# Retention and MoE on one core: chunk 1's loads over two hardware queues, chunk 2's k ahead of its q blocks, and M1(0) in four PSUM banks

## The chip, the core and the metric

The kernel runs on one core of a Trainium2 chip. The metric is the device time of one execution in microseconds (us), as a median over runs. Where a profile is read, times are microseconds from the start of its span, which is about 1.8 us shorter than the device time of the same execution. Engines go by the profile's names: PE is TensorE, PEld its weight loads, DVE VectorE, ACT ScalarE, POOL GpSimd, SP SyncE. A q behind a name (SPq, ACTq) marks the issue of DMAs; L419 is line 419 of that kernel's source, and x8 means eight instructions merged.

## The reference, cut to what matters

Two stages, one after the other. The first is a retention recurrence per batch and head, the second a two-layer MLP on its output:

```
B, H, S, D = 4, 8, 768, 64
state = gamma * state + k[t] v[t]^T            # per batch and head, gamma per head
y[t]  = q[t] . state / sqrt(D)
x     = y as (B*S, H*D) = (3072, 512)
out   = gelu_tanh(x @ w_in) @ w_out            # 512 -> 2048 -> 512
```

## The kernel before

The sequence is cut into six chunks of 128 tokens. For each chunk and each of the four batches the kernel makes the transposes T of q and k, the scores A, the output y and the state update S. Then the MLP runs over the chunk's 512 tokens: M1 (x @ w_in, 16 blocks "fc" of 128 columns, with gelu) and M2 (g @ w_out, four batches, each in units of four matmuls). "M1(1)" is M1 of chunk 1, "T(1,0)" the transposes of chunk 1, batch 0. The attention of the next chunk is woven into M1 and M2 of this one. PSUM is shared out in banks:

```python
BANKS = {"h": 2, "o": 2, "att": 4}        # M1, M2, attention: eight in all

def moe1_two(c, fp, t0, t1):              # two fc blocks for tokens t0..t1
    h_ps = bank("h", shape=(128, 2, B * C // 2), name="h_ps")
    for r in range(2):
        moe1_mm(c, 2 * fp + r, h_ps[:, r, 0:t1 - t0], t0, t1)
    gelu(g_tile(c, 2 * fp)[:, :, t0:t1], h_ps[:, :, 0:t1 - t0])
```

The loads of chunk 1 stand after M1(0) in the program. `hold` keeps the first q load back until the third piece of w_out has landed:

```python
hold("q", 1, 0, w_out_sb[2][0:1, 0, 0:1])
for fc in range(8, NF):                   # rest of M1(0)
    moe1(0, fc)
    if fc in (9, 11):
        load1(AC, "v", 1, (fc - 9) // 2)  # v(1,0), v(1,1) from ScalarE
...                                       # q and k by turns, all from SyncE
load1(AC, "v", 1, 2)
load1(AC, "v", 1, 3)
u = [units2(0, b, tag="ooho"[b]) for b in range(B)]   # M2(0)
run([u[i % 3][i // 3] for i in range(12)] + u[3], {8: [(preps, 1, 0)], 10: [(att_T, 1, 0), ...], ...})
load_blk("q", 2)                          # 16 DMAs of 64 KB, each for all four batches
for b in range(B):
    load1(SY, "k", 2, b)
...                                       # late outputs of chunk 0, v of chunk 2
```

From chunk 2 on q comes in blocks, which VectorE transposes itself, so POOL's scaling of q for any batch waits for all 16 block loads.

## Time and profile before

| | before |
|---|---|
| time | 216.12 us (216.09 to 216.35, 4 runs) |
| span of the profile | 215.2 us |
| TensorE (PE) busy | 206.6 us, 96% |
| PE's waits after 15 us | 0.79 (w_in), 0.24 (gelu), 1.37 (o bank) us |
| M1(1) starts, M2(1) starts | 52.55, 70.37 us |

The lines behind this are shown in the prediction. A bracket at the end of a timeline line gives the idle time just before it and what ended it.

### The profile page before, as it was taken

How to read it: one execution, taken by the hardware profiler on the slowest of the kernel's cores; microseconds unless marked ns; L12 is line 12 of the kernel's file. 1: busy time of each engine (PE TensorE's matmuls, PEld its weight loads, DVE VectorE, ACT ScalarE, POOL GpSimd, SP SyncE). 2: the span in 40 equal slices, each digit the busy share in tenths (PEclk: the TensorE clock that was granted, in tenths of full speed). 3: DMA queues.
4: the chain of work that ended last, by engine and by line, in shares of the span. 5: the costliest groups of instructions: out<-in, count | busy, mean ns of one | idle time of the engine just before them, and what ended most of it. 6: DMA issues, size and time to landing. Idle time of an engine off the chain costs nothing.

```text
span 215.2 us, 3935 instructions
## 1 busy us (share of the span) xinstructions
PE 206.6 (96%) x1551; PEld 113.5 (53%) x1551; DVE 86.4 (40%) x156; ACT 86.6 (40%) x149; POOL 96.5 (45%) x117
## 2 busy tenths in 40 slices
PE   7898999979999999999999999999999999999992
PEld 2466744447888655444545444545444544444461
DVE  5667000188755553217672235673235640100000
ACT  2456671054555223366123376123375113565110
POOL 2997100234279553569743799211499221100000
PEclk9999999999999999999999999999999999999998
DMA  6999999896799687899688998879920012100121
GB/s 153 288 234 207 206 205 229 198 250 111 155 227 282 109 161 146 173 286 187 101 159 166 280 207 130 125 147 221 296 57 0 0 61 88 49 0 0 52 97 49
DMA packets 124801, 32.78 MB, mean 152 GB/s; under 512 B 118064, under 2 KB 122928, under 8 KB 124784
## 3 DMA queue, kind: packets, MB, share of 16 engines
q1 hardware_dynamic: 107840, 20.48, 48.4%
q0 software_dynamic: 6112, 8.65, 17.2%
q10 hardware_dynamic: 10832, 3.41, 6.7%
q8 instruction: 12, 0.20, 0.4%
q14 instruction: 5, 0.04, 0.1%
HBM read 30.44 MB, written 6.29 MB: 171 GB/s over the span
## 4 chain that ended last, share of the span: by engine, by line
PE 76%; DMA 14%; POOL 3%; SPq 2%; ACT 1%; issue 0%; ACTq 0%; DVE 0%
PE o_ps L452 33%; PE h_ps L419 32%; DMA w_out<-in_moe_w_out_dram 9%; DMA k<-in_k_dram 5%; PE y_ps L307 3%; PE a_ps L272 3%; SPq L98 2%; PE y_ps L294 2%; PE s_ps L326 2%; POOL w_in L400 1%; PE qkT_ps L249 1%; POOL k L195 1%; DMA out_dram<-o_sb 1%; POOL w_out L409 1%; ACTq L98 0%
## 5 line engine op out<-in xcount | busy, mean ns | idle before, releaser
L452 PE MATMUL o_ps<-w_out,g 128*128 128x512 f16 (+1 forms) x400 | 88.1, 371 | 1.4 <-ACT o_sb L474 1.4
L419 PE MATMUL h_ps<-xT,w_in 128*128 128x512 f16 (+2 forms) x496 | 86.7, 331 | 1.1 <-DMA w_in<-in_moe_w_in_dram 0.8
L434 ACT ACTIVATE g<-h_ps 128x512 f16<-128x512 f32 (+1 forms) x98 | 57.5, 588 | 48.7 <-PE h_ps L419 48.6
L419 PEld LDWEIGHTS <-w_in 128*128 128x128 f16 x496 | 46.3, 98 | 37.0 <-DMA w_in<-in_moe_w_in_dram 1.0
L452 PEld LDWEIGHTS <-g 128*128 128x128 f16 x400 | 37.7, 98 | 40.2 <-issue 1.4
L285 DVE TENSOR_TENSOR a_sb<-a_ps,mask 128x512 f16<-128x512 f32 x48 | 30.1, 683 | 14.5 <-PE a_ps L272 14.4
L195 POOL TENSOR_TENSOR k<-k,cst 128x512 f16<-128x512 f32 x24 | 25.1, 1045 | 16.2 <-DMA k<-in_k_dram 16.1
L479 POOL DMA_DIRECT2D out_dram<-o_sb x17 | 9.6, 567 | 42.9 <-ACT o_sb L474 33.3
L474 ACT COPY o_sb<-o_ps 128x512 f32<-128x512 f32 x19 | 11.0, 586 | 41.6 <-PE o_ps L452 38.4
L352 POOL TENSOR_TENSOR stg<-st,cst 128x512 f32<-128x512 f16 x16 | 16.5, 1042 | 11.1 <-DVE st L343 9.7
L343 DVE TENSOR_TENSOR st<-s_ps,stg 64x256 f16<-64x256 f32 x32 | 13.5, 421 | 17.8 <-PE s_ps L326 17.2
L206 POOL TENSOR_TENSOR q<-q,cst 128x512 f16<-128x512 f32 x16 | 16.7, 1046 | 3.2 <-DMA q<-in_q_dram 3.2
L258 DVE STREAM_TRANSPOSE qkT<-q 128x512 f16<-128x512 f16 x16 | 11.2, 702 | 13.9 <-POOL q L206 13.7
L195 DVE TENSOR_TENSOR q<-q,cst 128x512 f16<-128x512 f32 x8 | 6.6, 826 | 21.9 <-DMA q<-in_q_dram 21.9
L231 ACT CAST xT<-y_ps 128x512 f16<-128x512 f32 x15 | 8.3, 588 | 12.0 <-PE y_ps L307 12.0
L206 POOL TENSOR_TENSOR kT<-kT,cst 128x512 f16<-128x512 f32 x12 | 12.5, 1044 | 0.5 <-issue 0.5
L171 PE MATMUL spin_ps<-zero 128*128 128x512 f16 x31 | 9.7, 456 | 1.3 <-DVE zero L139 1.3
L491 DVE COPY o_sb<-o_ps 128x256 f32<-128x256 f32 x1 | 0.4, 425 | 25.2 <-PE o_ps L452 25.2
L192 POOL CAST v<-v 128x512 f16<-128x512 f32 x16 | 9.6, 606 | 0.5 <-DMA v<-in_v_dram 0.4
L190 ACT CAST v<-v 128x512 f16<-128x512 f32 x7 | 4.3, 621 | 12.7 <-issue 10.8
L258 DVE STREAM_TRANSPOSE qkT<-kT 128x512 f16<-128x512 f16 x12 | 8.3, 694 | 2.6 <-POOL kT L206 2.6
L272 PE MATMUL a_ps<-qkT 64*128 64x128 f16 x192 | 8.1, 218 | 0.7 <-ACT qkT L231 0.7
(36 smaller groups left out, 95.1 us busy)
## 6 DMA issues: line engine op xcount, KB each, us to landing
k<-in_k_dram SPq DMA_DIRECT2D x22, 256.0 KB, 4.6
v<-in_v_dram SPq DMA_DIRECT2D x18, 256.0 KB, 4.7
out_dram<-o_sb POOLq DMA_DIRECT2D x17, 256.0 KB, 3.1
q<-in_q_dram SPq DMA_DIRECT2D x64, 64.0 KB, 2.7
kT<-in_k_dram SPq DMA_DIRECT2D x48, 64.0 KB, 2.8
w_out<-in_moe_w_out_dram POOLq DMA_DIRECT2D x4, 512.0 KB, 17.6
q<-in_q_dram SPq DMA_DIRECT2D x6, 256.0 KB, 5.5
v<-in_v_dram ACTq DMA_DIRECT2D x6, 256.0 KB, 7.6
```

Source lines behind the costliest of these rows:

```text
L171: nc.tensor.matmul(out=ps, lhsT=zero[:, 0:128], rhs=zero, start=True, stop=True)
L195: eng.tensor_tensor(out=t, in0=src, in1=cst[:, col:col + H].unsqueeze(2).broadcast_to([128, H, Dh]), op=ALU.mult,)
L206: nc.gpsimd.tensor_tensor(out=t, in0=ld_all((key, c))[:, b * NHP:(b + 1) * NHP].rearrange("p hp a d -> p (hp a) d"), in1=cst[:, col:col + ...
L258: nc.vector.transpose(out=t[:, i].rearrange("p hp t -> p (hp t)"), in_=blk16.pop((nm, c, b)).rearrange("p ha d -> p (ha d)"),)
L272: nc.tensor.matmul(out=ps[j][:, hp], lhsT=t[j * 64:(j + 1) * 64, 1, hp], rhs=t[j * 64:(j + 1) * 64, 0, hp], start=True, stop=True,)
L285: nc.vector.tensor_tensor(out=s, in0=ps[j], in1=mask[:, j], op=ALU.mult)
L343: eng.tensor_tensor(out=st[sl, :, b, sl], in0=s_ps[sl, :, sl], in1=stg[sl, :, b, sl], op=ALU.add,)
L352: nc.gpsimd.tensor_tensor(out=stg[:, :, b], in0=st[:, :, b], in1=cst[:, OG:OG + NHP].unsqueeze(2).broadcast_to([128, NHP, 128]), op=ALU.mult,)
L419: nc.tensor.matmul(out=out, lhsT=w_in_sb[wi][:, kc, wr * 128:(wr + 1) * 128], rhs=xT[c][:, kc, t0:t1], start=(kc == 0), stop=(kc == NHP - ...
L434: nc.scalar.activation(out=out, in_=in_, func=AF.Gelu_apprx_tanh, scale=1.0)
L452: nc.tensor.matmul(out=ps[:, n0:n1], lhsT=g_sb[c, fc // 2][:, fc % 2, b * C:(b + 1) * C], rhs=w_out_sb[fc // (NF // NO)][:, fc % (NF // NO ...
L474: nc.scalar.copy(out=o_sb, in_=ps)
```

## The change

The intent is to take out PE's last idle times before 60 us. The loads of chunk 1 go over both hardware queues so that nothing blocks ScalarE while it should empty M2's banks. M1(0) gets four banks and another order, so that it need not wait for a gelu or for w_in. Chunk 2's k goes ahead of its q blocks.

```diff
-    def moe1_two(c, fp, t0, t1):
-        h_ps = bank("h", shape=(128, 2, B * C // 2), name="h_ps")
+    def moe1_two(c, fp, t0, t1, tag="h"):
+        h_ps = bank(tag, shape=(128, 2, B * C // 2), name="h_ps")
...
-    moe1_two(0, 1, *t01)          # before y(0,2)
     mm_yc(0, 2, "o")
     mm_yi(0, 2)
     ev_Y(0, 2)
     mm_s(0, 2)
+    moe1_two(0, 1, *t01)
...
-    (pairs 1 to 3 in parts of 256 and 128 tokens, fc 8 to 15 whole)
+    moe1_two(0, 1, *t2, "o")
+    moe1_two(0, 0, *t3)
+    moe1_two(0, 1, *t3, "o")
...
-    for fc in range(8, NF):
+    for fc in range(4, NF):
...
-    load1(SY, "q", 1, 0)          # q and k by turns, all SyncE
-    load1(SY, "k", 1, 0)
-    ...
-    load1(AC, "v", 1, 2)
-    load1(AC, "v", 1, 3)
+    for b in range(B):
+        load1(SY, "q", 1, b)
+    for b in range(B - 1):
+        load1(AC, "k", 1, b)
+    load1(SY, "k", 1, 3)
+    load1(SY, "v", 1, 2)
+    load1(SY, "v", 1, 3)
...
-    load_blk("q", 2)
     for b in range(B):
         load1(SY, "k", 2, b)
+    load_blk("q", 2)
...                                # POOL: all k, all q, all v, in place of q and k by turns
```

More of the change, by code (lines that the diff above doesn't have):

```diff
@@ L573 @@
     moe1_two(0, 0, *t2)
-    moe1_two(0, 1, *t2)
-    moe1_two(0, 2, *t01)
+    moe1_two(0, 1, *t2, "o")
+    moe1_two(0, 0, *t3)
+    moe1_two(0, 1, *t3, "o")
     ev_S(0, 2)
     ev_S(0, 3)
-    moe1_two(0, 3, *t01)
-    moe1_two(0, 0, *t3)
-    moe1_two(0, 1, *t3)
-    for fp in range(2, 4):
-        moe1_two(0, fp, half, 2 * half)
     for b in range(B):
@@ L603, in preps @@
         prep1(AC, "v", c, b)
-    load1(SY, "q", 1, 0)
-    load1(SY, "k", 1, 0)
-    load1(SY, "q", 1, 1)
-    load1(SY, "k", 1, 1)
-    load1(SY, "q", 1, 2)
-    load1(SY, "k", 1, 2)
-    load1(SY, "q", 1, 3)
+    for b in range(B):
+        load1(SY, "q", 1, b)
+    for b in range(B - 1):
+        load1(AC, "k", 1, b)
     load1(SY, "k", 1, 3)
-    load1(AC, "v", 1, 2)
-    load1(AC, "v", 1, 3)
+    load1(SY, "v", 1, 2)
+    load1(SY, "v", 1, 3)
     u = [units2(0, b, tag="ooho"[b]) for b in range(B)]
@@ L636 @@
         load1(SY, "v", 2, b)
-    for b in range(B):
-        prep_blk("q", 2, b)
-        prep1(PO, "k", 2, b)
-    for b in range(B):
-        prep1(PO, "v", 2, b)
+    for nm in "kqv":
+        for b in range(B):
+            prep_blk("q", 2, b) if nm == "q" else prep1(PO, nm, 2, b)
     run(
```

## The prediction

> **What bounds the kernel now.** I read the page first, for who is busy.
>
> ```profile
> span 215.2 us, 3935 instructions
> PE 206.6 (96%) x1551; PEld 113.5 (53%) x1551; DVE 86.4 (40%) x156; ACT 86.6 (40%) x149; POOL 96.5 (45%) x117
> ```
>
> TensorE (PE) is busy 96% of the span, and the chain that ended last runs through its matmuls from 45 us to the end. So a microsecond taken out of PE's stream before that point is worth a microsecond at the end, unless a later wait takes it back. All that can be won is PE's idle time. The table of waits, cut to PE and to 15 to 62 us, lists all of it:
>
> ```profile
> PE o_ps L452 <- ACT o_sb L474: 1.4, 1, 1.4
> PE h_ps L419 <- DMA w_in<-in_moe_w_in_dram: 0.8, 1, 0.8
> PE h_ps L419 <- ACT g L434: 0.2, 1, 0.2
> ```
>
> The columns are total, count, longest. From 62 us on PE never waits. The timeline of PE shows where these three sit (start, length, instruction, idle before):
>
> ```profile
> 17.50 1.05 PE L419 MATMUL h_ps<-xT,w_in 128*128 128x256 f16 x8 [0.79 <-DMA w_in<-in_moe_w_in_dram]
> 18.48 0.41 PE L307 MATMUL y_ps<-a_sb,v 128*64 128x128 f16 x8
> 18.83 0.62 PE L326 MATMUL s_ps<-v,k 128*128 128x128 f16 x8
> ...
> 19.73 3.44 PE L419 MATMUL h_ps<-xT,w_in 128*128 128x128 f16 x40
> 23.41 9.26 PE L419 MATMUL h_ps<-xT,w_in 128*128 128x128 f16 x56 [0.24 <-ACT g L434]
> 32.51 9.66 PE L452 MATMUL o_ps<-w_out,g 128*128 128x512 f16 x44
> 42.00 0.39 PE L249 MATMUL qkT_ps<-iden,q 128*128 128x128 f16 x4
> ...
> 45.24 1.02 PE L452 MATMUL o_ps<-w_out,g 128*128 128x512 f16 x4 [1.37 <-ACT o_sb L474]
> ```
>
> The first wait is M1(0) (the first MoE matmul of chunk 0) for its second w_in piece, the second for a gelu to free an M1 bank, the third for ScalarE (ACT) to empty the bank that M2's last batch takes. Why ACT was late is in its timeline and in SyncE's:
>
> ```profile
> 38.77 0.85 SPq L98 DMA_DIRECT2D k<-in_k_dram  x1
> ...
> 43.02 1.02 ACTq L98 DMA_DIRECT2D v<-in_v_dram  x2
> 44.08 0.62 ACT L190 CAST v<-v 128x512 f16<-128x512 f32 x1 [10.78 <-issue]
> 44.61 1.07 ACT L474 COPY o_sb<-o_ps 128x512 f32<-128x512 f32 x2
> ```
>
> ACT's in-order stream holds two v loads ahead of the v cast and the copy. The order of instructions with their waits shows that the hardware-queue DMAs share eight completion semaphores, and that the first of these v loads waits for k(1,1), issued at 38.77, to land; the chain of waits has that at 42.94. ACT stands still for 10.78 us and then works off what was ready long before.
>
> Last, what feeds chunk 1: the timeline of GpSimd (POOL) shows when each k landed.
>
> ```profile
> 40.66 1.04 POOL L195 TENSOR_TENSOR k<-k,cst 128x512 f16<-128x512 f32 x1 [5.99 <-DMA k<-in_k_dram]
> 43.01 1.04 POOL L195 TENSOR_TENSOR k<-k,cst 128x512 f16<-128x512 f32 x1 [1.31 <-DMA k<-in_k_dram]
> ```
>
> k(1,0) is ready at 40.66 + 1.04 = 41.70, and PE takes its transpose at 42.00. This edge has only 0.3 us of slack, which matters below.
>
> **What the Trainium skill says.** "DMA: Bandwidth & Descriptors", section "Issuing engines are not separate DMA queues": DMAs from several engines run on the same 16 DMA engines, so a second queue saves only the time to start them. The trace half agrees: the prologue, on both queues, moved 284 GB/s from 7 to 12 us, and SyncE's queue alone reached 264 in 42 to 44, so the ceiling is near the same. But in 38 to 40 us the single queue gave only 119 GB/s, between one slow issue (2.99 us) and the next. Two queues should fill such holes, not raise the ceiling. The same page, "Queues, rings and completion order", says that each DMA engine takes turns between the queue rows that have work. That decides who comes first below; the trace agrees for the prologue, where loads of the two queues landed in turn about 0.9 us apart. "PSUM — Partial Sum Buffer", "Specifications (TRN2)", gives 8 banks per partition: the kernel holds 2 for M1, 2 for M2, 4 for attention, so M1 can have a third and fourth bank only by borrowing M2's, idle in this stage once y is evicted.
>
> **The change, part by part.**
> (a) M1(0) of pair 1 moves behind y(0,2) and s(0,2). Those are 0.35 us and 0.22 us of PE work (8 and 4 matmuls; the rows at 18.48 and 18.83 are spaced 0.35, and 8 s matmuls take 0.55 to the next). Their inputs are there by 16.8 us, and w_in only at 17.46. They fill 0.57 of the 0.79 us hole.
> (b) Four single-batch groups (8 matmuls of 128 columns each) come directly after one another, with M2's two banks for every second one, so four banks are in use and no gelu has to end first. Before, the 40 matmuls from 19.73 hold 2 x 8 x 0.109 + 3 x 8 x 0.055 = 3.06 us by their steady spacing, yet the next group starts 3.68 later: 0.6 us is really lost at the gelu, more than the 0.24 the table gives, since the ends of matmuls are modelled.
> (c) fc 4 to 7 run as 16 matmuls of 512 columns in place of 32 of 256: 16 x 0.216 = 3.45 against 32 x 0.109 = 3.49 us. That is nothing. Four 512-wide gelus stay four.
> Sum of (a) to (c): from 17.50, PE now has 0.98 (pair 1) + 0.22 (s) + 0.35 (y) + 1.76 (four single-batch groups) + 12 x 0.863 (fc 4 to 15) = 13.7 us, so M2(0) starts near 31.2 in place of 32.5: **1.3 us**. w_in and w_out pieces still come in time.
> (d) That lead meets the loads. M2(0) runs 11 units of 0.863 us and reaches T(1,0) (the transposes of chunk 1) at 40.7. k(1,0) now goes out from ACT behind v(1,0) and v(1,1), without the hold; but until 38 us the engines are full (277 GB/s from 36 to 38), and in front of it are the same bytes: w_out, two v, and q(1,0) by turns. So I put its landing at 40.6 again, k16 ready at 41.7, T(1,0) at about 41.75. Of the 1.3 us, **0.3 is left** here; 1.0 becomes a new wait of PE for k.
> (e) Behind ACT's k loads stand the v cast and the copies. The third, k(1,2), waits for q(1,0) to land (near 39.7), is out by 40.6, and the copy of M2's first batch ends by 41.7, while PE wants the bank at 43.4. The 1.37 us wait (1.44 by spacing: 43.80 to 45.24) is gone: **1.4 us**. From T(1,0) on PE has 10.55 - 1.44 = 9.1 us of work up to M1(1), which starts at 41.75 + 9.1 = 50.9 in place of 52.55: **1.7 us** so far.
> (f) The last v loads, now on SyncE behind q and k, each wait for an earlier q in the ring of semaphores: v(1,3) is issued near 45.1 and lands near 49.3 (4.2 us from issue, like k(1,1)), against 49.47 before. ACT casts it, copies u3 and evicts y(1,1) by 50.9: exactly when PE wants it. No gain and perhaps 0.2 lost.
> (g) Chunk 2: k loads first (4 x 0.9 us from 46), then 16 q blocks at 0.6 us each from 49.6, landed near 62. POOL now does k, then q: the second q is ready at 62 + 2 x 1.04 = 64.1, VectorE transposes and evicts by 65.0. PE wants A(2,0) and A(2,1) at 66.81 - 1.7 = 65.1. Cost 0 to 0.5; I take 0.2.
> Sum: 0.3 + 1.4 - 0.2 = 1.5, so 216.12 - 1.5 = **214.6 us**.
>
> **Rivals.** First, **the k and q loads keep up**: both rows alternate and k(1,0), already queued, goes ahead of q(1,0). It could land near 39.7; then step (d) keeps up to 1 us more and the time is 213.7. For it: the hole of 38 to 40 us. Against: full engines until 38. Second, **a new wait at the late loads**: v(1,3) or the q blocks come 1 us later than I reckon, as they are last in one queue. M1(1) or A(2,0) then gives back what was won: 215.4 to 215.8. For it: (f) and (g) have next to no slack. Third, **the bank borrowing backfires**: y(0,3)'s eviction on ACT ends at about 19.8 and PE comes for it at 19.9. A miss costs some 0.2 us, which (d) hides anyway.
>
> **Range and chances.** The sum is 1.5 us, the rivals reach from 0.3 to 2.5, so 213.5 to 215.8. Two per cent is 4.3 us, more than PE's whole idle time after 15 us; and no part adds PE work. So within 2%: 0.97, faster 0.02, slower 0.01.
>
> **What would show each step.** (a, b) M2(0) starts near 31.2, and PE's waits for w_in and g shrink to below 0.3 in sum. (d) PE waits about 1 us for POOL k before T(1,0). (e) PE no longer waits for ACT o_sb, and ACT's still stand ends before 41.5. (f) M1(1) starts at 50.9. (g) PE waits under 0.5 us for qkT near 65. I am wrong if M1(1) starts after 52, if PE shows no wait at T(1,0), or if A(2,0) waits over 1 us.

## The result, and the profile after

The changed kernel took **215.5 us** (215.3 to 216.06, 4 runs) against 216.12 us. The ratio is 0.9973, with a 95% interval of 0.9953 to 0.9993. Ratios are the mean time of one kernel's runs over that of the other's of the same rounds, so they are not quite the ratio of the medians. The gain is 0.6 us; 1.5 us were forecast. Within 2%, the prediction's first statement, was right.

The page of the kernel after, its span and busy times:

```profile
span 213.8 us, 3906 instructions
PE 205.9 (96%) x1535; PEld 111.8 (52%) x1535; DVE 85.8 (40%) x156; ACT 86.6 (41%) x149; POOL 96.9 (45%) x117
```

The span of this profile is 1.4 us shorter than that of before, near the forecast, while the times say 0.6. So at least one of the two executions profiled may not be typical.

The timeline of PE in the kernel after, the same places as in the prediction:

```profile
17.26 1.05 PE L419 MATMUL h_ps<-xT,w_in 128*128 128x256 f16 x8
...
18.81 12.32 PE L419 MATMUL h_ps<-xT,w_in 128*128 128x128 f16 x80
30.96 9.66 PE L452 MATMUL o_ps<-w_out,g 128*128 128x512 f16 x44
41.43 0.40 PE L249 MATMUL qkT_ps<-iden,q 128*128 128x128 f16 x4 [0.81 <-DVE q L195]
...
43.24 1.04 PE L452 MATMUL o_ps<-w_out,g 128*128 128x512 f16 x4
...
50.67 1.91 PE L419 MATMUL h_ps<-xT,w_in 128*128 128x256 f16 x16
...
64.68 0.40 PE L272 MATMUL a_ps<-qkT 64*128 64x128 f16 x8
65.56 0.40 PE L272 MATMUL a_ps<-qkT 64*128 64x128 f16 x8 [0.48 <-DVE qkT L233]
```

In the kernel before, the last two lines were one, A(2,0) and A(2,1) without a wait:

```profile
66.74 0.62 PE L272 MATMUL a_ps<-qkT 64*128 64x128 f16 x16
```

The reader is to see four things. The waits for w_in and gelu are gone, and M2(0) starts at 30.96 in place of 32.51. At 41.43 PE waits for q of chunk 1, so that T(1,0) comes only 0.57 us sooner than before. The 1.37 us wait for the o bank is gone (43.24). And a wait stands at A(2,1), 65.56, that the kernel before did not have.

ScalarE's and POOL's timelines in the kernel after bear on the last two:

```profile
31.17 9.79 ACTq L98 DMA_DIRECT2D k<-in_k_dram  x3
41.00 0.62 ACT L190 CAST v<-v 128x512 f16<-128x512 f32 x1 [9.24 <-POOL k L195]
41.53 1.07 ACT L474 COPY o_sb<-o_ps 128x512 f32<-128x512 f32 x2
```

```profile
62.33 4.07 POOL L206 TENSOR_TENSOR q<-q,cst 128x512 f16<-128x512 f32 x4 [4.25 <-DMA out_dram<-o_sb]
```

ScalarE is still held by its DMA issues, but until 41.0 and not 44.1, which is early enough for the bank. POOL's scaling of chunk 2's q starts at 62.33. The trace's landing records have the last of the 16 blocks at 61.94; POOL spends the 0.39 us between in the waits for eight semaphores. (The profile names an output DMA as releaser, but the program makes POOL wait for the blocks, and the outputs land later.) A(2,1) follows 3.23 us after POOL's start.

### The profile page after: what moved, and what is told of

The parts are those of the page before. It is cut to its first block, busy times and chain, and to the rows that moved or that the text cites. A ratio compares the mean times of both kernels' runs of the same rounds, so it can differ in the third digit from the quotient of the medians.

```text
span 213.8 us, 3906 instructions
## 1 busy us (share of the span) xinstructions
PE 205.9 (96%) x1535; PEld 111.8 (52%) x1535; DVE 85.8 (40%) x156; ACT 86.6 (41%) x149; POOL 96.9 (45%) x117
## 4 chain that ended last, share of the span: by engine, by line
PE 70%; DMA 16%; SPq 5%; POOL 4%; DVE 2%; issue 1%; ACT 0%; DVEq 0%
PE o_ps L452 34%; PE h_ps L419 27%; DMA w_out<-in_moe_w_out_dram 9%; SPq L110 4%; DMA k<-in_k_dram 3%; DMA q<-in_q_dram 3%; PE a_ps L272 2%; PE y_ps L307 2%; DMA out_dram<-o_sb 2%; PE y_ps L294 2%; PE s_ps L326 1%; POOL w_in L400 1%; POOL k L195 1%; PE qkT_ps L249 1%; DVE q L195 1%
## 5 line engine op out<-in xcount | busy, mean ns | idle before, releaser
L419 PEld LDWEIGHTS <-w_in 128*128 128x128 f16 x480 | 44.7, 98 | 37.0
L343 DVE TENSOR_TENSOR st<-s_ps,stg 64x256 f16<-64x256 f32 x32 | 13.5, 421 | 17.8 <-PE s_ps L326 17.2
L171 PE MATMUL spin_ps<-zero 128*128 128x512 f16 x31 | 9.2, 438 | 1.3 <-DVE zero L139 1.3
## 6 DMA issues: line engine op xcount, KB each, us to landing
w_out<-in_moe_w_out_dram POOLq DMA_DIRECT2D x4, 512.0 KB, 17.9
```

The lines of the kernel that those rows point to most:

```text
L343: eng.tensor_tensor(out=st[sl, :, b, sl], in0=s_ps[sl, :, sl], in1=stg[sl, :, b, sl], op=ALU.add,)
L419: nc.tensor.matmul(out=out, lhsT=w_in_sb[wi][:, kc, wr * 128:(wr + 1) * 128], rhs=xT[c][:, kc, t0:t1], start=(kc == 0), stop=(kc == NHP - ...
```

## The experiments

Eleven kernels ran in three sets, each set on one chip with its own runs of the kernel before. All results were correct.

```
set label                 median us   ratio to before   95% interval      before, median
1   e1_before_again       216.53      0.9995            0.9966 - 1.0023   216.55
1   e2_after_again        215.98      0.9966            0.9942 - 0.9990
1   e3_m1_only            217.13      1.0025            0.9996 - 1.0054
1   e4_loads_only         215.63      0.9953            0.9930 - 0.9975
2   e5_k2_split           214.45      0.9914            0.9896 - 0.9932   216.31
2   e6_k_early_split      214.69      0.9934            0.9908 - 0.9960
2   e7_q2_first           215.58      0.9962            0.9941 - 0.9984
2   e8_after_third        215.73      0.9975            0.9951 - 0.9999
3   e9_loads_split        215.17      0.9931            0.9917 - 0.9945   216.74
3   e10_outs_first        220.01      1.0123            1.0082 - 1.0165
3   e11_k2_split_again    215.14      0.9920            0.9904 - 0.9937
```

### e1 and e2: both kernels again

No edit. The first question was whether the profiles or the first four runs misled.

> The kernel before, unchanged, to see how far two profiles and two sets of runs of one program differ. The first profile of it was of an execution of 217.01 us while its timed runs gave 216.1. Theory A (the profile that the prediction was read from was an unlucky execution: TensorE came up to full clock at 5.2 us in it, 4.3 us in the profile of the changed kernel, so part of the 1.4 us between the two profiled spans is start-up): this profile has a span of 214.3 to 214.6 and reaches M1(1) about 0.2 to 0.9 us earlier than 52.55. Theory B (the profile was typical and the changed kernel's gain is lost somewhere in its ordinary runs): span again 215.2, M1(1) at 52.5. Ratio to before 1.000 for both.

> The changed kernel, unchanged, again with five rounds, for an interval narrow enough to tell 0.6 us from 1.4. Theory A: ratio 0.996 to 0.9975 (0.55 to 0.85 us), and the spread of its runs follows the start-up (time at which the clock is full). Theory B: single runs fall in two groups, some with the full 1.4 us and some with a lost bank or load wait near T(1,0) or A(2,0). If the prediction's size was right and the first four runs were unlucky: ratio 0.9930 to 0.9945.

The kernel before gave 0.9995 against itself, with single runs from 215.89 to 217.53 us, so one pair of profiles can lie a microsecond off. Its second profile, of an execution of 216.47 us, has a span of 214.7 and reaches M1(1) at 52.19: the profile that the prediction was read from (217.01 us) was indeed 0.3 to 0.9 us slower than the medians of the kernel before in the sets here. But theory A's reason falls. PE came to full clock at 5.26 us here and at 5.24 there, the same. And in the three profiles of the changed kernel (first, e2, e8) full clock comes at 4.30, 7.12 and 7.19 us and M1(0) starts at 14.92, 15.97 and 16.00, yet T(1,0) starts at 41.43, 41.26 and 41.29. In these, q(1,0) is loaded and scaled only at 41.38, 41.20 and 41.08, so the earlier start was lost in the wait for it, and the later ones came just in time. The changed kernel repeated its small gain, 0.9966. Its six runs (215.36 to 216.54) do not fall in two groups as theory B had it, but its profile, of an execution of 216.12 us, had the wait that theory B asked for, in PE's waits from 15 to 70 us:

```profile
PE a_ps L272 <- DVE qkT L233: 1.2, 2, 0.7
```

It is the wait at A(2,0) and A(2,1) again, 1.25 us now.

### e3 and e4: each half of the change alone

```diff
 e3: the diff above without its load lines (M1(0) part alone)
 e4: the diff above without its M1(0) lines (load part alone)
```

> Only the M1(0) part of the change (single batches in M2's banks too, pair 1 behind y(0,2) and s(0,2), fc 4 to 7 at 512 columns); all loads as before. My theory: M2(0) starts 1.3 us sooner, PE then waits for k of chunk 1 until 41.7 and for the o bank until about 45.1, so that M1(1) starts at most 0.2 us sooner than in the kernel before of the same run set: ratio 0.999 to 1.000. Rival (M1's lead is worth what it saves): ratio 0.994 to 0.9945.

> Only the load part of the change (q on SyncE, k on ScalarE, last v on SyncE, chunk 2's k ahead of its q blocks); M1(0) as before. My theory: the 1.4 us wait for the o bank goes and nothing takes its place, as PE reaches T(1,0) only at 42.0, after q and k: the same gain as the whole change or up to 0.2 us more, 0.6 to 1.4 us, ratio 0.9935 to 0.997. Rival (the gain comes from M1(0) and the loads only pass it on): ratio 0.999 or above.

The M1(0) part alone gave no gain, 1.0025. In its profile M2(0) starts at 31.48 and T(1,0) at 40.98, without the expected wait for k (ready at 40.90), and what had been won is waited off at the o bank, as expected:

```profile
44.70 1.50 PE L452 MATMUL o_ps<-w_out,g 128*128 128x512 f16 x4 [1.86 <-ACT o_sb L474]
```

M1(1) started at 53.68, later than expected. The reason shows in the windows of this run (length, busy time of PE, PEld, DVE, ACT and POOL, then the granted PE clock, DMA share and GB/s):

```profile
41.00:45.00 4.00, 2.14 (x23) 1.22 (x22) 3.26 (x4) 1.45 (x3) 1.40 (x2) 1.00 1.04 236
45.00:48.50 3.50, 3.50 (x16) 1.75 (x15) 1.29 (x2) 1.76 (x4) 1.39 (x2) 0.51 1.27 262
```

After that wait the clock of PE was halved for 3.4 us. Two of e3's six runs have a mean clock of 0.991 and 0.992 and took 217.94 and 218.06; the other four have 0.998 to 1.000 and took 216.5 to 217.4, the same as the kernel before. So without the clock drop the part is worth nothing alone, as expected. The load part alone gave 0.9953, 1.0 us: at least as much as the whole change (0.9966). The rival of e4 falls. Its profile, too, loses 0.23 us between M1(1) and M2(1) against the 17.65 us that a run without a wait takes, with POOL starting on q at 62.49.

### e5 to e8: what holds up A(2,0)?

The two profiles pointed at step (g). If chunk 2's q blocks take the gain back, two k loads that PE wants only at 68 us should go behind them:

```diff
 e5:
-    for b in range(B):
-        load1(SY, "k", 2, b)
+    load1(SY, "k", 2, 0)
+    load1(SY, "k", 2, 1)
     load_blk("q", 2)
+    load1(SY, "k", 2, 2)
+    load1(SY, "k", 2, 3)
...                                # POOL in the same order: k0, k1, all q, k2, k3, all v
```

> The changed kernel, but of chunk 2 only k(2,0) and k(2,1) load and are scaled ahead of its q blocks; k(2,2) and k(2,3), which TensorE wants only near 68 us, come after them. My theory now: in the changed kernel the q blocks land near 62 and TensorE waits for A(2,0) and A(2,1) 0.5 us (first profile) to 1.25 us (second), which takes back what M1(0) had won; here the q blocks land 1.8 us sooner, that wait goes, and TensorE goes from the start of M1(1) to M2(1) in 17.8 to 17.9 us (18.3 and 19.1 in the two profiles of the changed kernel). Timed: 0.4 to 1.2 us faster than the changed kernel of this set. Rival (the wait at A(2,0) is an accident of the two profiles, the loss lies elsewhere): within 0.2 us of the changed kernel.

e5 took 214.45 us, 0.9914: the mean of its runs is 1.23 us below that of the changed kernel on the same chip (e8: 215.70), at the upper end of what was expected, and its runs lie close together (214.08 to 214.84). POOL starts on q at 60.29, 2.0 us sooner than in the first profile of the changed kernel and 1.1 us sooner than in e8's, and PE takes A(2,0) and A(2,1) without a wait:

```profile
60.29 4.07 POOL L206 TENSOR_TENSOR q<-q,cst 128x512 f16<-128x512 f32 x4 [4.16 <-DMA k<-in_k_dram]
```

```profile
64.74 0.62 PE L272 MATMUL a_ps<-qkT 64*128 64x128 f16 x16
```

M1(1) to M2(1) is 50.72 to 68.37, 17.65 us, against 18.30 and 19.14 in the first two profiles of the changed kernel. The forecast of 17.8 to 17.9 was a little high. That e5 also moves two of POOL's scalings of k behind q is no rival: in the changed kernel POOL stands idle for 4.25 us before it starts on q.

The second idea was the wait at T(1,0):

```diff
 e6 = e5 and
-            load1(AC, "v", 1, (fc - 9) // 2)
+            load1(AC, "k", 1, (fc - 9) // 2)
...
-    for b in range(B - 1):
-        load1(AC, "k", 1, b)
+    load1(AC, "v", 1, 0)
+    load1(AC, "v", 1, 1)
+    load1(AC, "k", 1, 2)
```

> As e5, and ScalarE sends k(1,0) and k(1,1) during M1(0), v(1,0) and v(1,1) after it (their places exchanged), since q and k of chunk 1 hold up TensorE at T(1,0), 0.8 us in the first profile of the changed kernel, and v is not wanted for another 4 us. My theory: T(1,0) starts when TensorE gets there (about 9.5 us after M2(0) starts, 10.47 in the first profile of the changed kernel) or waits for q alone up to 0.3 us; 0.3 to 0.8 us faster than e5. Rival (the engines are full until 38 us whatever the order, q(1,0) lands as late as before): same as e5.

This missed. T(1,0) did start 9.50 us after M2(0) with no wait (so it did in e8 and e11 without this edit), but the time did not improve on e5 (0.9934 against 0.9914, intervals overlapping). Its profile had another wait, for the second piece of w_in, which landed at 18.58:

```profile
18.62 1.05 PE L419 MATMUL h_ps<-xT,w_in 128*128 128x256 f16 x8 [1.22 <-DMA w_in<-in_moe_w_in_dram]
```

The profile of e11, the kernel of e5, has the same wait at 1.1 us, and e10's at 1.4, so it is not e6's doing. Whether e6's order is worth anything is not settled.

```diff
 e7:
+    load_blk("q", 2)
     for b in range(B):
         load1(SY, "k", 2, b)
-    load_blk("q", 2)
...                                # POOL: q and k by turns again
```

> The changed kernel with the order of chunk 2 as before the change: q blocks ahead of k, and POOL taking q and k by turns. My theory: the blocks land near 58, k(2,0) only near 61 to 62, and TensorE waits 1 to 2 us at the transposes of k(2,0), T(2,0), instead of at A(2,0): 0.3 to 1.2 us slower than the changed kernel of this set. Rival: k is early enough and the time is that of e5 or better.

This missed too. Undoing the order of chunk 2 was not slower: 0.9962, against 0.9975 for the changed kernel of the set. q was ready early, and k(2,0), scaled at 59.27, was in time for T(2,0) at 60.44. Putting all of k ahead of q, one of the change's three parts, is worth nothing here. But e7 also leaves something open. With q early it should have come near e5, and its mean (215.43) is 1.0 us above. The profile caught one of its two fast runs (214.85 and 214.78; the other four took 215.48 to 215.95). In it k(2,0) and k(2,1) are ready 0.13 and 0.05 us before PE takes them, so a wait for k in the slower runs is likely; no profile of one shows it.

> The changed kernel once more, on the same chip as e5 to e7, to compare them with, and a third profile of it. Expected: ratio to the kernel before 0.9955 to 0.9975; in the profile TensorE waits at T(1,0) and at A(2,0) or A(2,1), 1 to 2 us in sum; from the start of M1(1) to M2(1) 18.3 us or more.

The ratio came as expected, 0.9975, at the edge of the range. The profile did not: it caught the fastest of the six runs (214.66 us; the others took 215.61 to 216.44), and PE had none of the expected waits. That is a miss that helps. Beside the other profiles of the same order of loads it gives the size of the wait by the start of POOL's q work:

```
kernel  this execution  POOL starts q  PE's wait at A(2,0), A(2,1)  M1(1) to M2(1)
e8      214.66 us       61.40          none                         17.65
after   215.59 us       62.33          0.48                         18.30
e2      216.12 us       62.93          1.25                         19.14
```

The times rise by 1.46 us from e8 to e2, M1(1) to M2(1) by 1.49: between these two executions of one program the difference is this wait. (From e8 to the first profile 0.65 of 0.93 us is the wait; M1(1) started 0.26 us later as well. The waits of the third column are some 0.2 us shorter than what the last column loses, as the ends of matmuls are modelled.) e8's five slower runs have no profile; that they waited here is inferred.

One check holds for every kernel here: from the start of M2(1) to the end of the span all thirteen profiles take 144.6 to 144.9 us. Whatever a profile wins or loses, clock drops included, is decided before M2(1).

### e9 to e11: the sum taken apart, and more of the suspect

```diff
 e9 = e5 without the M1(0) lines
 e10 = changed kernel and
-    load_blk("q", 2)
     for rows, o_sb in late:
         nc.sync.dma_start(out=rows, in_=o_sb)
+    load_blk("q", 2)
 e11 = e5 again
```

> e5 without the M1(0) part: the loads of the changed kernel, k(2,2) and k(2,3) behind the q blocks, M1(0) as before the change. It tells what M1(0)'s part is worth once the q blocks no longer hold up TensorE. My theory: the o bank wait of 1.1 to 1.4 us goes and nothing else, ratio 0.9935 to 0.9955, so e5 (0.9914 in its set) is 0.3 to 0.8 us faster. Rival (M1(0) gives nothing here either, all of e5's 1.85 us is loads): same as e5 within 0.2 us.

> The changed kernel with more of what I suspect: the three late writes of chunk 0's output go out ahead of chunk 2's q blocks on SyncE instead of behind them (some 1.4 us of issue, 0.75 MB). My theory: the q blocks land 1.4 to 2 us later, near 63.5 to 64.5, POOL starts on q at 63.5 or later, TensorE's waits at A(2,0) and A(2,1) grow by the same, and the kernel is 0.8 to 1.8 us slower than the changed one (ratio 1.001 to 1.006 to the kernel before). Rival (the q blocks have slack in ordinary runs): ratio as the changed kernel, 0.9965 to 0.9975.

> e5 again, for e9 to be compared with on one chip and to see whether its gain repeats: ratio 0.990 to 0.993 to the kernel before, and from M1(1) to M2(1) 17.6 to 17.7 us in the profile, which is what e5, e6 and e8 show without a wait.

e11 repeated e5, 0.9920, and 17.65 us from M1(1) to M2(1). POOL started on q at 61.37 in it, as late as in e8, and PE, late itself after the wait for w_in, came to A(2,0) at 65.23 and did not wait. e9 gave 0.9931, 1.5 us, a little more than expected. So the load part is worth 1.5 us once the q blocks are in time, and M1(0)'s part another 0.23 us (mean 215.24 against 215.01), which is nearer to the rival than to my 0.3 to 0.8 and not clear of noise.

e10 went the way expected and further. Here the profile itself names q as what POOL waits for, and PE waited 3.2 us:

```profile
65.44 4.06 POOL L206 TENSOR_TENSOR q<-q,cst 128x512 f16<-128x512 f32 x4 [7.04 <-DMA q<-in_q_dram]
```

```profile
67.74 0.40 PE L272 MATMUL a_ps<-qkT 64*128 64x128 f16 x8 [2.67 <-DVE qkT L233]
68.67 0.40 PE L272 MATMUL a_ps<-qkT 64*128 64x128 f16 x8 [0.53 <-DVE qkT L233]
```

It took 220.01 us, 1.0123. Four of its runs have a mean clock of 0.984 to 0.992, 219.75 to 220.71 us, and the profiled one shows the halved clock from 69.9 to 73.3 us. The two with a clock of 1.0 took 217.8 and 218.3. Even these are 1.4 us above their kernel before, some 2 us above the changed kernel (an estimate: its ratios of 0.9966 and 0.9975 put it at 216.0 to 216.1 in this set).

## Why the prediction was wrong

The time, 215.5, lay in the range, but 1.5 us of gain were forecast and 0.6 came. By its own steps:

- **(a), (b), (c), M1(0): the work was right, its start was not.** From the start of M1(0)'s pair 1 to M2(0) the new order takes 13.7 us in all nine profiles that have it, as forecast (15.0 to 15.25 in the four with the old order). But pair 1 starts at 17.26 to 18.89 in these nine, at w_in's landing where that is late (e6, e10, e11), and not always at 17.50. So M2(0) starts at 30.96 to 32.60. The forecast 31.2 was met in the first profile (30.96) and in e7's (31.26); the full lead of 1.3 us was partly luck.
- **(d), the lead lost at T(1,0): right in that the loads cap the lead, wrong in which.** T(1,0) came at 41.43 (41.75). PE waited 0.81 us there, for q and not for k as I had said: k landed first. In e2 and e8, where M2(0) started 0.8 us later, PE came as q was ready and did not wait, which the prediction had named as a sign of being wrong. What M1(0)'s part is worth in the end, 0.3 forecast, was 0.2 between e9 and e11, and nothing alone in e3.
- **(e), the o bank: right.** 1.4 us forecast. The wait is gone in all ten profiles with the new loads, and e9, the loads alone with the q blocks in time, gained 1.5 us.
- **(f), the last v: right.** M1(1) started at 50.67 (50.9), without a wait for it.
- **(g), chunk 2's q blocks: this is the step that failed**, "Cost 0 to 0.5; I take 0.2". The mechanism was seen, the size was not. PE waited 0, 0.5 and 1.25 us here in three profiles, and e5 against e8 puts the cost at 1.2 us on average. The terms were off as follows. The last block was to land near 62; it landed at 61.94 in the first profile, but at 61.01 and 62.53 in e8 and e2. POOL's start 0.39 us after that was left out. A(2,1) is free 3.2 us after POOL's start, where I had 3.0. And PE comes for A(2,0) at 64.4 (e8) to 64.7 (the first profile) and for A(2,1) 0.33 us later, in place of both at 65.1; the profile before, from which 65.1 came, takes 14.19 us from M1(1) to A(2,0), the first profile of the changed kernel and e8's 14.01 and 14.02. From these numbers I estimate that PE does not wait if POOL starts by about 61.5. With no slack a spread of the loads can only cost. The prediction's second rival, a new wait at late loads, is what happened, at A(2,0) and A(2,1).

With (g) measured the sum is 0.2 + 1.5 - 1.2 = 0.5 us, against 0.6, 0.7 and 0.5 in the three sets (216 us times 0.0027, 0.0034 and 0.0025). This is no independent proof: 0.2 + 1.5 is e11's gain and 1.2 what the same kernel, e5, gains over the changed one, so it shows that the sets agree. That the 1.2 us is this wait rests on e5, e8 and e10. What stays open is why the q blocks of one program land up to 1.5 us apart. The traces show where: SyncE starts issuing them at 49.34 in e8 and 50.14 in the first profile, a lag that is there from its first q load of chunk 1 on (34.20 and 34.81); in e2 it starts at 49.85 but takes 10.53 us for the 16, against 9.94 and 9.87.

The profile of the changed kernel alone would have hidden this: its 1.4 us came from setting a slow execution of the kernel before against a usual one of the changed kernel. The version that beats both is e5, 1.7 to 1.9 us faster than the kernel before in two sets.

## What to carry to other kernels

When loads stand in one queue, order them by the time at which each is wanted, not by tensor: two k loads ahead of q blocks that were wanted some 3 us sooner cost twice what the whole change gained. A step that ends just when it is wanted should be counted as a cost, since every run in which it is late loses and no run in which it is early wins. And when one stage is sped up, look at the next place where the loads set the pace: the lead is worth only the slack found there.

## What the Trainium skill lacked or had wrong

- "TensorE: Matmul & The Clock Gate", sections "What's actually happening" and "HAM oscillation — how this bites in real kernels", ties the halved clock to an idle window of about 3.4 us or to idle gaps over it (a later section speaks of frequent short idle gaps, without a length). The runs show it after less: 1.86 us of idle in e3, and 2.67 and 0.53 us in e10, were each followed by 3.4 us at half clock. A window with PE about half busy was enough in these runs (2.14 of 4.00 us in e3), though not in every one: four of e3's six and two of e10's six had mean clocks of 0.998 or more.
- The same page, "Back-to-back issue gap", gives 131 ns a matmul for a sustained stream with 512 columns. Here 64 of them took 13.81 us in both chains of waits, 216 ns each, which is what that section calls the isolated gap (elsewhere the page has 215.7 for back-to-back matmuls too).
- "DMA: Bandwidth & Descriptors", "Issuing engines are not separate DMA queues", calls the time to start a DMA usually small. Here the third of three 256 KB loads in a row took 2.99 us to issue from SyncE in the kernel before, where the first two took 0.37 and 0.58, and a k load lands 4.17 us after its issue. In the changed kernel three k loads held ScalarE's in-order stream for 9.79 us, the wait before the third included; the second alone took 6.15. No page that I read says how many DMAs a queue takes before its issuer is held.
